# Reordered loads, a second pair of decay buffers and a split last accumulation in a fused state-space scan and feed-forward kernel on one Trainium2 core

## The chip, the cores and the metric

The kernel runs on one core of one Trainium2 chip. The time is device microseconds (us) of one execution; the figure of a kernel is the median of its runs. The engines of the core run side by side, each through its own list of instructions in order: PE (TensorE, matmuls and transposes), DVE (VectorE), ACT (ScalarE), POOL (GpSimd) and SP (SyncE, which here only issues transfers). ACT and POOL issue transfers too, as instructions in their own lists. They wait for each other with semaphores.

## The reference

Two blocks follow each other. The first is a scan with decay (4 batches, 8 heads, 768 positions, 32 values a head, state size 16), the second a feed-forward block with 3072 tokens, width 256 and 2048 hidden values:

```python
for c in range(nc):
    xc, Bc, Cc = (x[:, :, sl], B[:, :, sl], C[:, :, sl])
    la = log_a[:, :, sl]
    cum = np.cumsum(la, axis=-1)
    L = np.exp(cum[:, :, :, None] - cum[:, :, None, :]) * causal
    M = np.einsum('bhin,bhjn->bhij', Cc, Bc) * L
    y_intra = np.einsum('bhij,bhjd->bhid', M, xc)
    y_inter = np.einsum('bhin,bhnd->bhid', Cc, state) * np.exp(cum)[:, :, :, None]
    y[:, :, sl] = y_intra + y_inter
    Bx = np.einsum('bhjn,bhjd->bhjnd', Bc, xc) * decay_from_j[:, :, :, None, None]
    state = decay_full[:, :, None, None] * state + np.sum(Bx, axis=2)
x = y.transpose(0, 2, 1, 3).reshape(B * S, H * D)
h = x @ w_in
out = (h * (1.0 / (1.0 + np.exp(-h)))) @ w_out
```

`w_in` and `w_out` arrive as 64-bit floats.

## The kernel before, in words

**Units and pairs.** The 3072 tokens are cut into 12 units of 256 tokens (three to a batch), and the units into 6 pairs. A unit is first scanned: that gives `XF`, its 256x256 input of the feed-forward block. The first pair (units 0 and 1) then goes through the feed-forward block with plain fp32 matmuls on 256 columns (`f_s1`, line 508, and `f_s2`, line 521). Pairs 1 to 5 go through it with operands split in three (`h`, `l` and `d` parts, matmuls of lines 536, 544, 576, 577 and 590) in 80 steps (`step`), 16 to a pair, while the next pair is scanned in between.

**The steps of a scan.** For unit u: `f_T` or `f_TP` transpose B and C (`f_TP` on PE, into one of two PSUM tiles of the tag `h`); `f_T2` makes `ce` on ACT; `f_P` makes `PFX`, the running product of the decays along a chunk of 64, from the tile `pz` (scan on DVE, line 328); `f_C` makes `CW` = transposed C times `PFX` (line 391), which is the last reader of the PSUM tile of `f_TP`; `f_E1` or `f_Ek` make the decay matrix `E` (line 341) from `ab`; `f_B` makes `BT`; `f_G` and `f_D0` are small matmuls (419, 407); `f_S`, `f_SM` carry the state; `f_M` multiplies `E` by the products; `f_Y` and `f_X` (459, 468, 478) give `XF`.

**The decays.** Units 0 and 1 get `ab` by a matmul (`f_Ab`) and `pz` from `pa01`, a broadcast load clamped by `f_P0`. From unit 2 on both are broadcast loads from two arrays in DRAM, `a_in` and `a_zero`, that the kernel itself writes: `acl` holds all decays, `f_A2` clamps them on DVE (265), copies them with a zero column to `acz` (266, 267) and stores both (268, 269). The first column of `a_in` is stored early (274). `load_pa` (line 105, one transfer) and `load_ab` (line 112, four transfers) read them back. There is one `pz` tile for all units.

**The weights.** 16 tiles of 512 KB (`raw`, line 185; 8 of `w_in`, 8 of `w_out`) go through six buffers, `quad`. Each becomes fp32 in five steps: `w_size` on ACT (191, 194), `w_bits` on DVE (199, 201, 202) and an add on POOL (207), which gives `w32`. Tile n may be loaded once `w_bits(n-6)` has read its buffer.

**The order.** The order in which instructions are written is the order on each engine. It is written out by hand: the calls from line 641 on for units 0 and 1, then the table `steps`, whose rows read (unit, weight tile, what to do after that `f_s1`): `b5` is `w_bits(5)`, `s6` is `w_size(6)`, `r11` loads tile 11, `2:T` is the transposing of unit 2, `2:C12B` its `f_C`, `f_E1` twice and `f_B`, and so on. The hidden values of `f_s1` leave the two PSUM tiles `h` by a Silu on ACT (`gT`, 511). All loads but `bn` of unit 0 are issued by SP, in one list; a tiny transfer `mark` (255) holds tile 5 back until tile 3 has landed.

**The end.** `step(80)` to `step(82)` finish the last pair: `s2` (576, 577) adds to the two accumulators `OA[P][0]` and `OA[P][1]`, `s2_d` (590) to `B2`; `f_sum2` (598, ACT) reads `B2`, `f_end` (622, DVE) joins them, and `store` transposes (633) and stores (635) on SP and ACT.

Of the kernel before, what the change touches and what calls it, by code (L numbers as in the profile page):

```python
# [33 lines left out]
def kernel(  # L34
# [48 lines left out]
    sc.tile([128, 40], FP32, name="pad")  # L83
# [15 lines left out]
    ab, bn, tbc, xt = ({} for _ in range(4))  # L99
# [4 lines left out]
    def load_pa(u, q):  # L104
        q.dma_start(out=pz.rearrange("p c t -> p (c t)"),
                    in_=a_in[:, 4 * u:4 * u + 4].rearrange("h (o c) t -> h o (c t)", o=1).to_broadcast([H, N, 4 * Q + 4]))
# [7 lines left out]
    def load_n(u, i, q):  # L114
        b, t0 = at(u)
        if i == 0:
            t = bn[u] = (block("bn0")[:, 0:256].rearrange("p (k h n) -> p k h n", k=2, h=H) if u < 2 else
                         loads.tile([128, 2, H, N], FP32, name="bn"))
        else:
            t = tbc[u] = block("tbc0")[:, 0:256].rearrange("p (k h n) -> p k h n", k=2, h=H)  # L120
        for k in range(2):
            q.dma_start(out=t[:, k], in_=(B, C)[i][b, :, t0 + 128 * k:t0 + 128 * k + 128].rearrange("h p n -> p h n"))  # L122
# [111 lines left out]
    pa01 = block("pa01")  # L234
    pz = const.tile([128, 4, Q + 1], FP32, name="pz")
    one = const.tile([128, 4, Q + 1], FP32, name="one")
    load_t(0, 1, nc.sync)
    load_n(0, 0, nc.scalar)
    nc.sync.dma_start(out=pa01, in_=bass.AP(tensor=a.tensor, offset=a.offset, ap=[[S, H], [0, N], [1, 2 * UT]]))
    load_x(0, nc.sync)  # L240
    for n in range(3):
        load_w(n, nc.sync)
# [4 lines left out]
    acl, acz = (block(n).rearrange("p (h t) -> p h t", t=Q) for n in ("acl", "acz"))  # L247
# [4 lines left out]
    mark = const.tile([1, RAW - 5], U32, name="mark")  # L252
    for n in range(3, RAW):
        if n > 4:
            nc.sync.dma_start(out=mark[:, n - 5:n - 4], in_=raw[n - 2][0:1, 0, 0, 0:1])
        load_w(n, nc.sync)

# [4 lines left out]
    def f_A2():  # L262

        r = slice(0, NC0 * batch)
        nc.vector.tensor_scalar(out=acl[r], in0=acl[r], scalar1=1.0, scalar2=1e-6, op0=ALU.min, op1=ALU.max)
        nc.vector.tensor_copy(out=acz[r], in_=acl[r])
        nc.vector.memset(acz[r, :, 0:1], 0.0)
        nc.sync.dma_start(out=a_in[:, :, 1:].rearrange("h c t -> c h t"), in_=acl[r])
        nc.sync.dma_start(out=a_zero, in_=acz[r])
# [4 lines left out]
    nc.sync.dma_start(out=a_in[:, :, 0:1].rearrange("h c t -> c h t"),  # L274
                      in_=misc[:NC0 * batch, 0:H].rearrange("p (h t) -> p h t", t=1))
# [17 lines left out]
    nc.vector.memset(pz[:, :, 0:1], 0.0)  # L293
    nc.vector.memset(one, 0.0)
    nc.vector.memset(one[:, :, 0:1], 1.0)
    for c in range(2):
# [5 lines left out]
    ident = const.tile([128, 128], FP32, name="ident")  # L302
    nc.vector.memset(ident, 0.0)
    nc.gpsimd.affine_select(out=ident, in_=ident, pattern=[[-1, 128]], compare_op=ALU.not_equal,
                            fill=1.0, base=0, channel_multiplier=1)

    diag = const.tile([128, H, Q], FP32, name="diag")
    nc.vector.tensor_copy(out=diag, in_=diag1.to_broadcast([128, H, Q]))
# [5 lines left out]
                            fill=0.0, base=N - 1, channel_multiplier=-1)  # L314
    par = const.tile([128, 2], FP32, name="par")
# [6 lines left out]
    def f_P0(u):  # L322
        src = pa01[:, UT * u:UT * u + UT].rearrange("p (c t) -> p c t", t=Q)
        nc.vector.tensor_scalar(out=pz[:, :, 1:], in0=src, scalar1=1.0, scalar2=1e-6, op0=ALU.min, op1=ALU.max)

    def f_P1(u):
        PFX[u] = sc2.tile([128, 4, Q + 1], FP32, name="pfx")
        nc.vector.tensor_tensor_scan(out=PFX[u].rearrange("p c t -> p (c t)"),
                                     data0=pz.rearrange("p c t -> p (c t)"),
                                     data1=one.rearrange("p c t -> p (c t)"), initial=0.0,  # L330
                                     op0=ALU.mult, op1=ALU.add)

    def f_P(u):
        if u < 2:
            f_P0(u)
        f_P1(u)
# [25 lines left out]
    def f_B(u, engine=nc.vector):  # L362
        BT[u] = sc.tile([128, 2, H, N], FP32, name="BT")
        engine.tensor_tensor(out=BT[u], in0=bn[u], in1=E[u][:, :, :, Q - 1:Q].to_broadcast([128, 2, H, N]),
                             op=ALU.mult)
# [23 lines left out]
    def f_C(u):  # L389
        CW[u] = sc.tile([128, UT], FP32, name="cw")  # L390
        nc.vector.tensor_tensor(out=CW[u].rearrange("p (c t) -> p c t", t=Q),  # L391
                             in0=CT.pop(u).rearrange("p (c t) -> p c t", t=Q), in1=PFX[u][:, :, 1:], op=ALU.mult)
# [6 lines left out]
    def f_D0(u):  # L399
        last = u % UPB == UPB - 1  # L400
        bt = BT.pop(u).rearrange("p k h n -> p k (h n)")
        xc = xt[u].rearrange("p k h d -> p k (h d)")
        d = [new_dp(u)[:, c, 256:384].rearrange("p (k x) -> p k x", k=2) for c in range(2)]
        for t in range(3 if last else 4):
            k, c = divmod(t, 2)
            for g in range(4):
                nc.tensor.matmul(out=d[c][32 * g:32 * g + 32, k],  # L407
                                 lhsT=bt[64 * c:64 * c + 64, k, 32 * g:32 * g + 32],
                                 rhs=xc[64 * c:64 * c + 64, k, 64 * g:64 * g + 64], start=True, stop=True,
                                 tile_position=(64 * c, 32 * g), skip_group_check=True)  # L410
        BX[u] = d

# [154 lines left out]
    def s2(s):  # L567
# [5 lines left out]
        gh, gl = GH.pop(s), GL.pop(s)  # L573
        for m in range(2):
# [65 lines left out]

    f_T(0, 1)
    for e in range(2):
        f_T2(0, e)
    f_Ab(0, 0)
# [4 lines left out]
    busy(2, 10)  # L649
    f_Ek(0, 0)  # L650
    f_Ek(0, 1)
    f_B(0)
    f_D0(0)
    f_P(0)
    f_C(0)
# [8 lines left out]
    busy(3, 18)  # L664
# [13 lines left out]
    w_bits(2, 2)  # L678
    f_P(1)
    f_C(1)  # L680
    f_G(1)
# [8 lines left out]
    for n in range(6, 9):  # L690
        load_w(n, nc.sync)
    load_bcx(2)
# [6 lines left out]
    load_pa(2, nc.sync)  # L699
    load_ab(2, nc.sync)  # L700
    load_w(10, nc.sync)
    load_bcx(3, "cx")
    w_size(5)

    def stage(u, what):
        for c in what:
            if c == "L":
                load_unit(u)
            elif c == "A":
                load_pa(u, nc.sync)  # L710
                load_bcx(u, "b")
                load_ab(u, nc.sync)
# [39 lines left out]
    def todo(text):  # L752

        for step in text.split():
            if ":" in step:
# [6 lines left out]
    steps = ((1, 0, ""), (0, 3, "b5 r11 s6"), (1, 1, "b6 s7"), (1, 2, "b7 s8"), (1, 3, "b8"), (0, 4, "2:T"),  # L762
             (1, 4, "2:P"), (0, 5, "2:C12B s9 3:A r12 r13"), (1, 5, "2:D b9 r14 r15 s10"), (0, 6, "2:SsM"), (1, 6, "b10 s11"),
             (0, 7, "2:Y b11 s12 3:T"), (1, 7, "3:PC12B b12 s13 h0 l0"))
# [3 lines left out]
    for text in ("m0 3:D 4:L 3:SsM 2:h h1 l1 2:l 2:d d0 b13 s14", "m1 3:Y 3:h h2 l2 d1 b14 s15", "m2 3:l 3:d d2 b15 h3 l3",  # L768
                 "m3 p0 d3 h4 l4 4:T", "m4 h8 l8 d4 h5 l5 d8", "m5 d5 h9 l9 d9"):
        todo(text)  # L770
# [14 lines left out]
    def step(s):  # L785
# [14 lines left out]
        if s == last + 1:  # L800
            s2(t)
# [3 lines left out]
        if s == last + 2:  # L805
            s2(t)
            f_end(NP - 1)
            return
# [11 lines left out]
        if t >= 0 and not ends:  # L820
            s2(t)
# [58 lines left out]
```

## Time and profile before

| | |
|---|---|
| time, median of 3 runs (lowest, highest) | 338.35 us (338.19, 340.29) |
| the profiled execution: its time | 339.9 us |
| its span | 338.0 us |
| mean granted TensorE clock in it | 0.986 |
| PE busy | 322.8 us (96%) |
| DVE busy | 252.4 us (75%) |
| ACT busy | 218.6 us (65%) |
| POOL busy | 69.1 us (20%) |
| moved by DMA | 30.87 MB, mean 91 GB/s |

The span is the time between the first and the last instruction that the profiler saw; 1.9 us of the profiled execution lie around it. All start times below are counted from the start of the span. A busy PE is not a PE at its peak: at a lower granted clock the same matmuls are busy for longer.

### The profile page before, as it was taken

The numbers are of one execution on the slowest core, as the hardware profiler recorded it, in microseconds if no ns is written. First come the engines' busy times: TensorE is split into PE (matmuls) and PEld (weight loads), VectorE is DVE, ScalarE is ACT, GpSimd is POOL, SyncE is SP. The second block draws the span as 40 slices with busy tenths as digits, with TensorE's granted clock in tenths as the row PEclk, the third lists the DMA queues.
The fourth block names the chain that finished last, engine by engine and source line by source line (L and its number), as shares of the span: only waits on it lengthen the run. The fifth ranks groups of instructions, "written<-read, shape, count | busy, mean of one in ns | idle before, by whom it ended". The sixth has DMA issues, their size and how long they took to land.

```text
span 338.0 us, 7790 instructions
## 1 busy us (share of the span) xinstructions
PE 322.8 (96%) x3145; PEld 256.4 (76%) x3146; DVE 252.4 (75%) x420; ACT 218.6 (65%) x417; POOL 69.1 (20%) x66
## 2 busy tenths in 40 slices
PE   8879599999999999999999999999999999999992
PEld 4558478888878778778788778788778788888881
DVE  7998558997677888996965996865996854674443
ACT  3656535956478898767666666767667756666651
POOL 3226313257001222231202230202240202000000
PEclk9999969999999999999999999999999999999998
DMA  6968878795674584154330154420343000020003
GB/s 127 224 211 211 191 185 206 222 170 108 114 150 67 101 157 89 46 112 75 71 78 0 50 107 85 101 40 0 66 104 52 2 2 0 0 49 17 0 2 62
DMA packets 97290, 30.87 MB, mean 91 GB/s; under 512 B 82230, under 2 KB 88374, under 8 KB 97254
## 3 DMA queue, kind: packets, MB, share of 16 engines
q1 hardware_dynamic: 90758, 25.78, 34.1%
q0 software_dynamic: 2304, 4.20, 7.2%
q10 hardware_dynamic: 4192, 0.39, 0.9%
q8 instruction: 25, 0.41, 0.5%
q14 instruction: 11, 0.09, 0.1%
HBM read 22.82 MB, written 3.34 MB: 77 GB/s over the span
## 4 chain that ended last, share of the span: by engine, by line
PE 85%; SPq 8%; DMA 4%; DVE 1%; issue 1%; ACT 0%; DVEq 0%; ACTq 0%
PE hp L544 23%; PE b L590 11%; PE hp L536 11%; PE oa L576 11%; PE oa L577 11%; PE oa L521 8%; PE hp L508 4%; SPq L122 4%; DMA raw<-in_moe_w_in_dram 3%; PE gy L468 2%; PE gy L419 2%; PE gy L459 2%; DMA pz<-a_in 1%; PE gy L407 1%; SPq L185 1%; SPq L145 1%
## 5 line engine op out<-in xcount | busy, mean ns | idle before, releaser
L538 ACT ACTIVATE hp<-hp 128x512 f32<-128x512 f32 x80 | 46.6, 583 | 72.1 <-PE hp L536 72.0
L558 DVE TENSOR_TENSOR gl<-g,gh 128x512 fp32r<-128x512 f32 x62 | 42.7, 689 | 52.2 <-ACT gh L554 49.1
L544 PE MATMUL hp<-xh,wh 128*128 128x512 f32 x160 | 65.2, 407 | 0.0
L562 DVE SCALAR_TENSOR_TENSOR gd<-gh,g 128x512 fp32r<-128x512 f32 x80 | 59.5, 747 | 5.2 <-ACT gh L554 5.2
L544 PE MATMUL hp<-xl,wl 128*128 128x512 f32 x160 | 62.6, 391 | 0.0
L576 PE MATMUL oa<-gh,wh 128*128 128x512 f32 x160 | 62.5, 391 | 0.0
L577 PE MATMUL oa<-gl,wl 128*128 128x512 f32 x160 | 62.4, 390 | 0.0
L558 POOL TENSOR_TENSOR gl<-g,gh 128x512 fp32r<-128x512 f32 x18 | 29.2, 1623 | 121.9 <-ACT gh L554 121.9
L554 ACT ACTIVATE gh<-g 128x512 fp32r<-128x512 f32 x80 | 50.5, 632 | 2.8
L536 PE MATMUL hp<-xd,wd 128*128 128x512 f32 x160 | 49.5, 391 | 0.0
L552 ACT ACTIVATE g<-hp 128x512 f32<-128x512 f32 x80 | 47.5, 593 | 0.5 <-PE hp L544 0.5
L590 PE MATMUL b<-gd,wd 128*128 128x512 f32 x160 | 44.4, 390 | 0.0
L508 PE MATMUL hp<-xf,w 128*128 128x256 f32 x128 | 32.8, 411 | 5.1 <-DVE cw L391 3.3
L544 PEld LDWEIGHTS hp<-xh,wh 128*128 128x128 f32 x160 | 30.0, 188 | 9.1 <-ACT hp L538 2.5
L536 PEld LDWEIGHTS hp<-xd,wd 128*128 128x128 f32 x160 | 30.0, 188 | 6.7
L576 PEld LDWEIGHTS oa<-gh,wh 128*128 128x128 f32 x160 | 30.0, 188 | 6.4
L590 PEld LDWEIGHTS b<-gd,wd 128*128 128x128 f32 x160 | 30.0, 188 | 6.5 <-DVE o L616 0.3
L577 PEld LDWEIGHTS oa<-gl,wl 128*128 128x128 f32 x160 | 30.0, 188 | 6.3
L508 PEld LDWEIGHTS hp<-xf,w 128*128 128x128 f32 x128 | 25.5, 205 | 11.3 <-issue 3.6
L544 PEld LDWEIGHTS hp<-xl,wl 128*128 128x128 f32 x160 | 30.1, 188 | 5.2
L207 POOL TENSOR_TENSOR w<-wu,wv 128x512 uint32<-128x512 uint32 (+1 forms) x20 | 23.3, 1174 | 45.6 <-DVE wv L202 41.7
L521 PE MATMUL oa<-gT,w 128*128 128x256 f32 x128 | 29.0, 381 | 0.0
(81 smaller groups left out, 375.2 us busy)
## 6 DMA issues: line engine op xcount, KB each, us to landing
ab<-a_zero SPq DMA_DIRECT2D x40, 128.0 KB
raw<-in_moe_w_in_dram SPq DMA_DIRECT2D x8, 512.0 KB
raw<-in_moe_w_out_dram SPq DMA_DIRECT2D x8, 512.0 KB
wl<-w POOLq DMA_DIRECT2D x16, 256.0 KB, 4.2
xt<-in_x_dram SPq DMA_DIRECT2D x24, 128.0 KB
out_dram<-ot SPq DMA_DIRECT2D x44, 64.0 KB
bn<-in_B_dram SPq DMA_DIRECT2D x22, 64.0 KB
tbc<-in_C_dram SPq DMA_DIRECT2D x22, 64.0 KB
```

The costliest lines, as they stand in the source:

```text
L508: nc.tensor.matmul(out=hp[:, i], lhsT=two(w32[j])[:, kc, 128 * i:128 * i + 128], rhs=two(XF[u])[:, kc], start=(kc == 0), stop=(kc == KC - 1))
L521: nc.tensor.matmul(out=OA[0][m][:, UT * u:UT * u + UT], lhsT=two(w32[8 + j])[:, i, 128 * m:128 * m + 128], rhs=two(GT[u, j])[:, i], start= ...
L536: nc.tensor.matmul(out=HP[s], lhsT=two(WD[f // 2])[:, kc, 128 * (f % 2):128 * (f % 2) + 128], rhs=XD[P][:, kc], start=(kc == 0), stop=Fals ...
L538: nc.scalar.activation(HP[s], HP[s], AF.Copy, scale=-HALF / UP)
L544: nc.tensor.matmul(out=HP[s], lhsT=two(w[f // 2])[:, kc, 128 * (f % 2):128 * (f % 2) + 128], rhs=x_[P][:, kc], start=False, stop=(kc == KC ...
L552: nc.scalar.activation(G[s], HP.pop(s), AF.Silu, scale=UP)
L554: nc.scalar.activation(GH[s], G[s], AF.Copy, scale=DOWN)
L558: engine.tensor_tensor(out=GL[s], in0=G[s], in1=GH[s].bitcast(FP32), op=ALU.subtract)
L562: nc.vector.scalar_tensor_tensor(out=GD[s], in0=GH[s].bitcast(FP32), scalar=1.0 + 1.0 / HALF, in1=G.pop(s), op0=ALU.mult, op1=ALU.subtract)
L576: nc.tensor.matmul(out=OA[P][m], lhsT=two(WH[n])[:, r, ms], rhs=gh, start=(f == 0), stop=False)
L577: nc.tensor.matmul(out=OA[P][m], lhsT=two(WL[n])[:, r, ms], rhs=gl, start=False, stop=(f == NF - 1))
L590: nc.tensor.matmul(out=B2[P][:, m], lhsT=two(WD[n])[:, r, 128 * m:128 * m + 128], rhs=gd, start=(fresh and s == tiles[0]), stop=True, skip ...
```

## The change

It has six parts; lines of the new file are a few higher than those of the old one.

1. **Unit 0 and the start.** The load of the decays of units 0 and 1 is split: unit 0's half goes first on ACT's queue, unit 1's half stands after weight tile 0 on SP's. `pz1` is a tile of its own for unit 1. The clamp and scan of unit 0 are done before its C is transposed; unit 0's `f_C` and unit 1's clamp go to POOL, the copy `diag` to ACT, the memset of `ident` to POOL. `f_B` and `f_D0` of unit 0 are done for k = 0 and k = 1 in turn. There are fewer idle matmuls (`busy`).
2. **Decay arrays.** `acz` and its two DVE instructions go: `a_zero` is stored straight from `acl` without its first column. Both stores go to ACT's queue; the first columns of both arrays are stored from POOL.
3. **Loads of unit 2.** C before weight tile 6 on SP, B on ACT's queue after `f_B(1)`, and `pz`, `ab`, x between weight tiles 6, 7 and 8. `mark` goes.
4. **Loads of unit 3.** `pz3` and a `bn` block of its own; both are loaded before `steps`, and `ab` after `f_B(2)`.
5. **`steps`.** Unit 2 is worked on three to four groups earlier, unit 3 two to three; weight steps stand later.
6. **The last pair.** Its last three `s2` do accumulator 0 first, and accumulator 1 of all three afterwards.

```diff
     def load_pa(u, q):
-        q.dma_start(out=pz.rearrange("p c t -> p (c t)"),
+        PZ[u] = pz if u != 3 else block("pz3")[:, 0:4 * Q + 4].rearrange("p (c t) -> p c t", c=4)
+        q.dma_start(out=PZ[u].rearrange("p c t -> p (c t)"),
...
-    nc.sync.dma_start(out=pa01, in_=bass.AP(tensor=a.tensor, offset=a.offset, ap=[[S, H], [0, N], [1, 2 * UT]]))
     load_x(0, nc.sync)
-    for n in range(3):
+    load_w(0, nc.sync)
+    load_a(1, nc.sync)
+    for n in range(1, 3):
         load_w(n, nc.sync)
...
     for n in range(3, RAW):
-        if n > 4:
-            nc.sync.dma_start(out=mark[:, n - 5:n - 4], in_=raw[n - 2][0:1, 0, 0, 0:1])
         load_w(n, nc.sync)
+    load_n(2, 1, nc.sync)
...
-        nc.vector.tensor_copy(out=acz[r], in_=acl[r])
-        nc.vector.memset(acz[r, :, 0:1], 0.0)
-        nc.sync.dma_start(out=a_in[:, :, 1:].rearrange("h c t -> c h t"), in_=acl[r])
-        nc.sync.dma_start(out=a_zero, in_=acz[r])
+        nc.scalar.dma_start(out=a_in[:, :, 1:].rearrange("h c t -> c h t"), in_=acl[r])
+        nc.scalar.dma_start(out=a_zero[:, :, 1:], in_=acl[r, :, 1:])
...
+    def f_A0():
+        for t in (a_in[:, :, 0:1].rearrange("h c t -> c h t"), a_zero[:, :, 0:1]):
+            nc.gpsimd.dma_start(out=t, in_=misc[:NC0 * batch, 0:H].rearrange("p (h t) -> p h t", t=1))
...
+    f_P0(0, nc.vector)
+    f_P(0)
     f_T(0, 1)
     for e in range(2):
         f_T2(0, e)
+    f_C(0, nc.gpsimd)
+    f_P0(1, nc.gpsimd)
+    f_A0()
...
     f_G(0)
-    busy(2, 10)
     f_Ek(0, 0)
+    f_B(0, slice(0, 1))
+    f_D0(0, (0, 1))
+    busy(1, 10)
     f_Ek(0, 1)
-    f_B(0)
-    f_D0(0)
-    f_P(0)
-    f_C(0)
+    f_B(0, slice(1, 2))
+    f_D0(0, (2, 3))
...
     f_B(1)
-    w_bits(2, 2)
+    load_n(2, 0, nc.scalar)
     f_P(1)
     f_C(1)
+    w_bits(2, 2)
...
     f_A2()
-    for n in range(6, 9):
-        load_w(n, nc.sync)
-    load_bcx(2)
+    load_w(6, nc.sync)
+    load_pa(2, nc.sync)
+    load_ab(2, nc.sync)
+    load_w(7, nc.sync)
+    load_x(2, nc.sync)
+    load_w(8, nc.sync)
...
-    load_pa(2, nc.sync)
-    load_ab(2, nc.sync)
     load_w(10, nc.sync)
     load_bcx(3, "cx")
+    load_pa(3, nc.sync)
+    load_bcx(3, "b")
...
-    steps = ((1, 0, ""), (0, 3, "b5 r11 s6"), (1, 1, "b6 s7"), (1, 2, "b7 s8"), (1, 3, "b8"), (0, 4, "2:T"),
-             (1, 4, "2:P"), (0, 5, "2:C12B s9 3:A r12 r13"), (1, 5, "2:D b9 r14 r15 s10"), (0, 6, "2:SsM"), (1, 6, "b10 s11"),
-             (0, 7, "2:Y b11 s12 3:T"), (1, 7, "3:PC12B b12 s13 h0 l0"))
+    steps = ((1, 0, ""), (0, 3, "b5 r11 s6"), (1, 1, "2:PTC1"), (1, 2, "b6 r12 s7 2:2Ba"), (1, 3, "b7 r13 s8"),
+             (0, 4, "2:DSsM"), (1, 4, "b8 r14 s9"), (0, 5, "2:Y b9 r15 s10"), (1, 5, "3:TPC"), (0, 6, "3:12B s11"),
+             (1, 6, "b10 s12 h0 l0"), (0, 7, "3:DSsM 2:h"), (1, 7, "b11 s13"))
...
         if s == last + 1:
-            s2(t)
+            s2(t, (0,))
             s2_d([t, t + 1])
             f_sum2(NP - 1)
             return
         if s == last + 2:
-            s2(t)
+            s2(t, (0,))
+            for i in range(LAG):
+                s2(last - LAG + i, (1,))
             f_end(NP - 1)
```

## The prediction
> **What bounds the kernel now.** I read the page's forty slices first, then the chain of waits, then PE, SP, DVE and ACT in order of time. In the slices, PE is full from the sixth on and its clock falls once:
>
> ```profile
> PE   8879599999999999999999999999999999999992
> PEclk9999969999999999999999999999999999999998
> ```
>
> From 43 us to 331 us the chain is PE alone. Time can be won before 43 us, in the slow clock behind it, and at the end. PE in order of time (start, duration):
>
> ```profile
> 25.43 8.90 PE L508 MATMUL hp<-xf,w 128*128 128x256 f32 x40 [0.47 <-ACT xf L478]
> 35.04 1.97 PE L508 MATMUL hp<-xf,w 128*128 128x256 f32 x8 [0.71 <-ACT gT L511]
> ...
> 42.96 6.44 PE L508 MATMUL hp<-xf,w 128*128 128x256 f32 x16 [3.28 <-DVE cw L391]
> ...
> 50.31 5.45 PE L508 MATMUL hp<-xf,w 128*128 128x256 f32 x24
> ```
>
> PE stands 3.28 us for `cw` of unit 2, because the PSUM tile of the transposed C is free only after it. The next 16 matmuls take 6.44 us, where 24 take 5.38 us in the chain (1.79 per group of 8, so 3.58 for 16): 2.86 us more. The windows of 2 us show why (after the length: busy time of PE, PEld, DVE, ACT, POOL; then the granted clock, DMA share, GB/s):
>
> ```profile
> 40.00:42.00 2.00, 0.00 (x0) 0.00 (x0) 0.44 (x1) 0.32 (x1) 0.00 (x0) 0.93 0.99 260
> 42.00:44.00 2.00, 1.04 (x3) 0.89 (x4) 1.87 (x4) 0.00 (x0) 0.00 (x0) 0.50 0.97 240
> 46.00:48.00 2.00, 2.00 (x6) 1.56 (x5) 0.07 (x1) 1.25 (x3) 0.00 (x0) 0.50 0.76 145
> ```
>
> So this stall costs 3.28 + 2.86 = 6.1 us. DVE and SP show its source:
>
> ```profile
> 41.56 0.70 DVE L328 TENSOR_TENSOR_SCAN pfx<-pz,one 128x260 f32<-128x260 f32 x1 [3.63 <-DMA pz<-a_in]
> ```
> ```profile
> 28.88 6.07 SPq L122 DMA_DIRECT2D bn<-in_B_dram  x2
> 35.05 1.15 SPq L145 DMA_DIRECT2D xt<-in_x_dram  x2
> 36.31 0.88 SPq L185 DMA_DIRECT2D raw<-in_moe_w_out_dram  x1
> 37.23 0.64 SPq L105 DMA_DIRECT2D pz<-a_in  x1
> ```
>
> `a_in` was stored at 23.68, but its reader is issued at 37.23: it stands behind tiles 6 to 9 and the loads of unit 2 in SP's list. The DMA engines are not the limit (share 0.71 to 0.89 between 10 and 60 us, and 24 GB/s in one slice near 33 us).
>
> The end: PE is done at 331.3, and the tail hangs on ACT's sum.
>
> ```profile
> 330.45 1.09 ACT L598 ACTIVATE sum<-b 128x512 f32<-128x512 f32 x2 [3.33 <-PE b L590]
> ```
>
> [...] line 201 takes 0.43 us alone and 1.38 beside POOL's line 207.
>
> **The change part by part.** Times are of the profiled execution (339.9 us, span 338.0), 1.55 above the median of the runs; I subtract the gain from the median.
>
> *Ceiling of the stretch.* From 25.43 to the first line 544 at 82.98 are 57.55 us. PE's work in it: 13 groups x 1.79 = 23.3; `f_s2` 3.45 + 3.65 + 7.10 + 6.91 = 21.1; G and D0 0.98 + 1.01; Y 1.41 + 1.29; one `f_TP` 0.85; line 536 0.46. Sum 50.4, so 7.1 us are lost, 6.1 of them above. None of this work is removed.
>
> *Start (part 1).* DVE loses behind unit 0's second E: clamp 0.28, scan 0.70, `cw` 0.42; the first two reappear in front of E, where DVE waits 0.76 for `hm` and where `hm` now comes before `ident`. `diag` (0.43), `ident` (0.17) and unit 1's clamp (0.29) leave DVE, as do 0.42 + 0.07 in part 2. Half of `f_B` goes before the second E; two small instructions for one, at most +0.1. Sum on DVE about 0.9 earlier at unit 1's M. But XF of unit 1 is made on ACT, behind two new transfer issues there (0.32 each, as SP's rows 268 and 269) and `w_size(4)`: I take 0.3 of 0.9. ACT's `diag` (0.6 as line 511) is hidden beside the wait of 2.02 for `ct`. POOL is idle 8.60 us before 13.15: `f_C`, clamp, and two stores of 4-byte items fit (0.9 to 1.0 per issue as line 220; at POOL's 1.6 against DVE's 0.7 in line 558, `f_C` costs 1.0). If they don't fit, `w32` of tile 0 and with it PE are late: -0.9 to +1.0, taken 0.3 gain. [...] Moving `w_bits(2)` behind P and C of unit 1 (0.7 to 1.13, and 0.42) makes group (0,2) up to 1.3 late, hidden because Y of unit 1 waits for DVE's M then (1.33).
>
> *Loads of unit 2 (parts 2, 3).* On ACT, B's two issues take 1.09 (row ACTq L122), inside ACT's wait of 2.52 before `sm`. ACT issues the `a_in` store at about 23.5. Landing: SP's last output store (issue ended 334.7) had landed by 338.0, so at most 3.3 us: at 26 to 27 SP is let past `pz`. Tiles 3 to 6 and C are ahead in the DMA engines; without `mark` (3.3 us of SP's waiting, 23 GB/s from 21 to 22.5) they go back to back, tile 6 by about 27. So `pz` lands by 27 + 2 to 4.3 (4.3 is its value now, behind a tile) = 29 to 31. DVE reaches its scan behind `w_bits(5)` at about 29, scan and `cw` end 31 to 32.5. PE wants that PSUM tile when group (1,2) is done: 25.1 + 3 x 1.79 + 0.85 + 1.79 = 33.1. **The stall goes**; its cover is about 1 us. The four `ab` (2.41 to issue) land by 32 to 33; E 2 x 1.2, `w_bits(6)` 1.6 to 2.4 between, BT 0.42: 36 to 37, against PE's arrival behind G at 36.7 + 0.6 = 37.3: 0.
>
> *What is late next.* Tile 7 is issued after `ab`, at about 29.5, tile 8 after x at about 31; at 4.3 to 4.5 each (tile 3: 16.91 to 21.24) they land at 34 and 36 to 37. `w_size(7)` and `w_size(8)` stand on ACT in front of the Silu of the group before last, and with two `h` tiles PE waits for that. Silu of (0,4) ends 38.5 to 40 against PE's need at 39.5. I take 0.7 us of new waits, ends 0 and 3. [...]
>
> *Unit 3 and `steps` (parts 4, 5).* `pz3`, two `bn`, four `ab`, x and C have landed by about 45, E of unit 3 runs from about 46. ACT has some 22 us of work in the 27 us of the groups, DVE about 23: cover, but thin. From m0 on, DVE has `w_bits(11..15)` still to do (5 x 1.6 to 2.4), PE 21.1 us of `f_s2`: hidden. Taken 0.3, ends 0 and 2.
>
> Sum: 6.1 + 0.5 (half of the other 1.0) + 0.3 - 0.7 - 0.3 = 5.9 us.
>
> *The end (part 6).* From the last line 544 (325.82) 24 matmuls remain, 0.227 each. `b` needs all its own and what stands before it: 20 now (ends 330.37), 16 after: 0.91 earlier. `gd` of the last tile (328.44) is ready at that place. ACT's sum, DVE's `o` and transpose follow one another; PE still ends at 331.3, before the second `o` wants it (331.5). Gain 0.9.
>
> Total 6.8: span 331.2, profiled execution 333.1, against the median 338.35 - 6.8 = **331.5**.
>
> **The rivals.**
> *A (0.70):* as above, 329.0 (7.1 + 0.9 + 0.9 and a little) to 333.5.
> *B (0.17): half is given back.* ACT's waits for tiles 7 to 10, or DVE beside POOL, open new PE gaps of 3 to 4 us in several pieces. For it: ACT is strictly in order and all weights move later. Against: 20% spare in the stretch. 335, within 334 to 336.
> *C (0.07): slower, SP stuck behind the stores.* If the store of `a_in` lands T later than 27, everything behind `pz` in SP's list is T later. With 0.7 of cover, PE loses T - 0.7[...]. It decides from T = 4.6 (6.8 gone); T = 8 gives 8 - 0.7 + 2.9 - 6.8 = +3.4: 341.8. For it: 4-byte and 252-byte items, a wait never seen here. Against: the output stores landed within 3.3.
> *D (0.06): it doesn't do it.* The stall stays, with another last release (`bn` or `pz` as late): only the end's gain, 337.5.
>
> **How the numbers follow.** 1% is 3.4 us (below 334.97, above 341.73), about what a measurement tells apart. Faster: A and over half of B, 0.81. Same: the rest of B, D and the mild part of C, 0.13. Slower: 0.06. The range 329 to 336 leaves out C, D and some 0.05 of A's and B's edges.
>
> **What would show it.** Right: no wait of line 508 on `cw`, clock 1.00 from 42 to 48 us, `pz` issued near 27, line 544 first near 77, ACT's sum 0.9 us closer behind PE. Wrong: a PE gap at groups (1,4) or (0,5) behind ACT and a weight DMA, SP held past 30 us at `pz`, or a second dip in the clock.

## The result, and the profile after

| | before | after |
|---|---|---|
| median of 20 runs each, side by side | 338.88 us | 341.07 us |
| lowest, highest | 337.17, 343.15 | 339.06, 343.89 |
| span of the profiled execution | 338.0 | 340.4 |
| PE's first split matmul (line 544, after 550) | 82.63 | 85.58 |
| mean granted TensorE clock | 0.986 | 0.988 |

The ratio is 1.0062 (95% interval 1.0037 to 1.0088): a little slower, inside 1%, where 331.5 us was predicted. The row of the first split matmul holds the answer: up to PE's first split matmul (the texts of the experiments call it the first scatter) 2.95 us are lost; from there to the end 0.55 us are won.

The forty slices of the changed kernel, PE and its clock:

```profile
PE   7877994999999999999999999999999999999993
PEclk9997999899999999999999999999999999999999
```

The old dip in slice 6 is gone. In its place there are two: one in slice 4 (25.5 to 34 us) and a hole in PE in slice 7 with a milder dip behind it. PE in order of time names both (start, duration; in brackets the idle time before, and what ended it):

```profile
27.26 7.13 PE L514 MATMUL hp<-xf,w 128*128 128x256 f32 x24 [2.37 <-ACT xf L484]
35.08 5.45 PE L514 MATMUL hp<-xf,w 128*128 128x256 f32 x24 [0.25 <-ACT gT L517]
...
59.24 0.65 PE L411 MATMUL gy<-xt,BT 64*32 64x64 f32 x32 [4.48 <-DVE BT L368]
59.82 3.44 PE L514 MATMUL hp<-xf,w 128*128 128x256 f32 x8
```

The wait of 3.28 us for `cw` is gone, as forecast: the second line waits 0.25 us, for a Silu. **Gap 1** is the first line: PE stands 2.37 us for `XF` of unit 1, where it stood 0.47, and the 24 matmuls behind it take 7.13 us at a granted clock of 0.66 from 28 to 30 us and 0.50 from 30 to 32 us, where 24 take 5.45 at 1.00 (the second line). **Gap 2** is the third: 4.48 us for `BT` of unit 3, then 3.44 us for 8 matmuls at 0.50 from 60 to 62 us (1.99 at 1.00). Behind gap 1 the clock costs 1.7 us, behind gap 2 about 1.5.

ACT ahead of gap 1. `ACTq` is the issue of a transfer in ACT's list:

```profile
23.60 0.50 ACTq L273 DMA_DIRECT2D a_in<-acl  x1
25.55 0.67 ACTq L274 DMA_DIRECT2D a_zero<-acl  x1
26.27 0.66 ACT L192 ACTIVATE wu<-raw 128x512 f32<-128x512 f32 x1 [2.16 <-DMA tbc<-in_C_dram]
26.84 0.65 ACT L484 ACTIVATE xf<-gy 128x256 f32<-128x256 f32 x2
```

Line 192 is the first half of tile 4's size. The bracket puts ACT's 2.16 us down to the load of C, though the instruction reads tile 4; and the issue of the `a_zero` store, ahead of it in the list, began 1.45 us after the other store's had ended. Two suspects then stand ahead of `XF`: the store and tile 4. Before, the same size ran at 24.10 without a wait and `XF` at 25.00.

Gap 2, first in SP's list, then on DVE:

```profile
35.02 4.33 SPq L186 DMA_DIRECT2D raw<-in_moe_w_out_dram  x3
...
42.29 3.35 SPq L146 DMA_DIRECT2D xt<-in_x_dram  x2
45.69 1.57 SPq L106 DMA_DIRECT2D pz<-a_in  x1
...
50.84 2.41 SPq L113 DMA_DIRECT2D ab<-a_zero  x4
```
```profile
51.31 0.42 DVE L395 TENSOR_TENSOR cw<-ct,pfx 128x256 f32<-128x256 f32 x1
56.39 2.34 DVE L344 TENSOR_TENSOR_SCAN E<-ab,diag 128x512 f32<-128x512 f32 x2 [4.65 <-DMA ab<-a_zero]
```

DVE had everything for `E` of unit 3 but `ab`, whose four loads SP issued only from 50.84 on: they stand behind tiles 8 to 10, C, x, `pz` and B of unit 3 and two more tiles. `E` begins 10 us after the forecast 46.

The end went as worked out:

```profile
332.86 1.09 ACT L606 ACTIVATE sum<-b 128x512 f32<-128x512 f32 x2 [2.42 <-PE b L598]
```

ACT waits 2.42 us there instead of 3.33.

### The profile page after: what moved, and what is told of

The parts are those of the page before. It is cut to its first block, busy times and chain, and to the rows that moved or that the text cites. A ratio compares the mean times of both kernels' runs of the same rounds, so it can differ in the third digit from the quotient of the medians.

```text
span 340.4 us, 7774 instructions
## 1 busy us (share of the span) xinstructions
PE 322.7 (95%) x3136; PEld 256.8 (75%) x3136; DVE 251.7 (74%) x416; ACT 219.0 (64%) x418; POOL 71.4 (21%) x71
## 3 DMA queue, kind: packets, MB, share of 16 engines
HBM read 22.82 MB, written 3.34 MB: 77 GB/s over the span
## 4 chain that ended last, share of the span: by engine, by line
PE 83%; DMA 5%; SPq 5%; DVE 3%; ACT 1%; issue 1%; DVEq 0%; ACTq 0%
PE hp L550 23%; PE b L598 11%; PE hp L542 11%; PE oa L584 10%; PE oa L585 10%; PE oa L527 8%; PE hp L514 3%; SPq L123 2%; PE gy L474 2%; PE gy L465 2%; DMA tbc<-in_C_dram 2%; PE gy L425 2%; DMA ab<-a_zero 1%; DMA pz<-a_in 1%; DVE E L344 1%; SPq L186 1%
## 5 line engine op out<-in xcount | busy, mean ns | idle before, releaser
L344 DVE TENSOR_TENSOR_SCAN E<-ab,diag 128x512 f32<-128x512 f32 x24 | 28.4, 1209 | 4.8 <-DMA ab<-a_zero 4.7
```

The lines of the kernel that those rows point to most:

```text
L344: nc.vector.tensor_tensor_scan(out=E[u].rearrange("p k h t -> p (k h t)")[:, Q * g0:Q * (g0 + n)], data0=t.rearrange("p g t -> p (g t)"), ...
```

## The experiments

Each row is a profiled span, the first split matmul in it, and the ratio of the medians to the kernel before (95% interval).

| | built on | span | first split matmul | ratio |
|---|---|---|---|---|
| e1_stores_behind_xf | after | 339.5 | 84.80 | 1.0081 (1.0054 to 1.0109) |
| e2_ab3_on_pool | after | 335.4 | 80.37 | 0.9967 (0.9947 to 0.9987) |
| e4_tail_alone | before | 335.9 | 81.50 | 0.9990 (0.9969 to 1.0012) |
| e5_pz2_ahead | before | 336.3 | 81.01 | 0.9977 (0.9958 to 0.9997) |
| e6_b2_on_sp | e2 | 334.2 | 79.64 | 0.9910 (0.9883 to 0.9938) |
| e7_stores_on_pool | e2 | 333.9 | 78.92 | 0.9944 (0.9924 to 0.9965) |
| e8_clock_kept | e2 | 335.2 | 80.19 | 0.9948 (0.9925 to 0.9971) |
| e9_unit3_first | e7 | 334.6 | 80.14 | 0.9991 (0.9965 to 1.0017) |
| e10_stores_on_pool_alone | after | 341.1 | 86.22 | 1.0044 (1.0025 to 1.0063) |
| e11_x3_last | e7 | 334.7 | 80.19 | 0.9965 (0.9946 to 0.9984) |
| e12_tiles_later | e7 | 336.1 | 81.58 | 0.9970 (0.9952 to 0.9987) |
| e13_b2_sp_and_pool | e7 | 336.5 | 82.11 | 0.9921 (0.9894 to 0.9949) |
| e14_tiles_on_pool | e7 | 335.3 | 80.47 | 0.9961 (0.9927 to 0.9995) |
| e15_tile4_ahead | e7 | 336.2 | 81.29 | 0.9934 (0.9915 to 0.9954) |
| e16_mark_back | e2 | 338.0 | 82.19 | 1.0024 (0.9996 to 1.0051) |

One profiled execution and the median can differ by more than these edits do: e9's profile is the fastest of its 14 executions, those of e10 and e13 are the slowest of theirs. Single waits vary too. e7, e9, e11 and e12 are the same program up to the load of tile 8, yet PE's wait for `XF` of unit 1 reads 0.47, 0.47, 1.20 and 0.47 us, and its wait for the Silu at some 32 us 0.53, 0.67, 0.40 and 1.47. So a wait read from one trace is good to about 1 us. Each verdict below rests on a named wait first, and on the ratio second.

### Gap 2: a place in SP's list

```diff
-                load_ab(u + 1, nc.sync)
+                load_ab(u + 1, nc.gpsimd)
```

> The changed kernel, but the four loads of ab of unit 3 are issued by POOL instead of SP. Theory (place in SP's list): ab of unit 3 lands at 56.3 us because it stands behind x, pz, B and two weight tiles; POOL can issue it at about 41 to 45 us, it lands by 50, PE's gap of 4.48 us before the small matmuls of line 411 goes with the half clock behind it (8 matmuls in 3.44 us instead of 1.8), and the kernel is about 6 us faster than the changed one (near 335 us). Rival (bandwidth): the DMA engines are full there, ab lands no earlier than 54 or the weights land later instead, and less than 2 us are gained.

The issue on POOL, `E` of unit 3 on DVE, and PE behind it:

```profile
41.55 2.12 POOL L113 DMA_DIRECT2D ab<-a_zero  x4
```
```profile
52.47 2.33 DVE L344 TENSOR_TENSOR_SCAN E<-ab,diag 128x512 f32<-128x512 f32 x2
```
```profile
55.32 0.46 PE L411 MATMUL gy<-xt,BT 64*32 64x64 f32 x32 [0.16 <-DVE BT L368]
```

No bracket on `E`: it runs as soon as DVE is there, and 4.48 us of PE's wait have become 0.16. The half clock behind it went too (1.00 from 56 to 64 us). The span fell by 5.0 us and the ratio from 1.0062 to 0.9967, clear of both intervals; the median is 337.13, where 335 was forecast. Gap 2 is the place of `ab` in SP's list; this is shown. Gap 1 stayed (2.25 us, then 7.13 us for 24 matmuls).

Do the two gaps add up? This one mends gap 1 alone: both stores on POOL, tile 4's size behind `XF`, `ab` of unit 3 left on SP.

> The changed kernel, with both stores issued by POOL and the first half of tile 4's size behind XF, and nothing else: the four ab of unit 3 stay in SP's list. It says whether the two gaps add up. Theory (they lie in series, and the second is set by SP's list, whose place in time doesn't move with PE): the gap ahead of unit 1's first group falls from 2.37 to 0.5 and its 24 matmuls from 7.13 to 5.4, so PE is 3.5 us earlier at 34 us; but E of unit 3 still begins when ab lands near 55 to 56, so PE's wait for BT of unit 3 grows from 4.48 to 6.5 to 8 us, and the span stays at 339 to 340.5. Rival (SP's list is let go earlier because the stores land earlier and the tiles come free earlier): ab of unit 3 lands 1.5 to 3 us earlier too, the wait stays at 4 to 5.5, and the span is 337 to 338.5.

```profile
58.84 0.68 PE L411 MATMUL gy<-xt,BT 64*32 64x64 f32 x32 [5.30 <-DVE BT L368]
```

Gap 1 fell to 0.47 us, but PE gave part back to Silus (0.31, 1.05 and 0.62 us), came to the line of gap 2 1.2 us earlier (53.5 instead of 54.8), and waited 5.30 us there instead of 4.48: `E` began at 55.98 (56.39 in the changed kernel), and the span was 341.1. The forecast growth (6.5 to 8) was too large, the reading right: the gaps lie in series. Until the second is mended, mending the first gains nothing that the ratios can tell apart (1.0044 against 1.0062, with overlapping intervals).

### Gap 1: which thing held ACT

The first try left both stores on ACT but put them, and tile 4's size, behind `XF` of unit 1.

> The changed kernel, but ACT makes XF of unit 1 before it issues the stores of a_in and a_zero and before the first half of weight step 4. Theory (ACT's list): PE's gap of 2.37 us in front of the first group of unit 1 and the half clock behind it (24 matmuls in 7.13 us instead of 5.38) come from XF standing behind a store that waits in ACT's list; here the gap is under 0.6 us, the clock stays at 1.00 between 27 and 33 us, and the kernel is about 4 us faster than the changed one (near 337 us), less whatever the stores' later landing (about 2 us) takes back at pz. Rival (DMA): the weights are late because the loads of B of unit 2 share the DMA engines with tiles 3 to 5; then the gap only moves to the next group, which needs tile 3's or 4's w32, and the kernel gains under 1.5 us.

```profile
25.12 1.38 ACTq L276 DMA_DIRECT2D a_in<-acl  x1
26.53 1.48 ACTq L277 DMA_DIRECT2D a_zero<-acl  x1
```
```profile
30.95 1.99 PE L517 MATMUL hp<-xf,w 128*128 128x256 f32 x8 [1.96 <-ACT gT L520]
```

`XF` came in time (0.47 us), but ACT then stood in the two store issues (1.38 and 1.48 us), and PE waited 1.96 us for the Silu behind them and 1.81 for `BT` of unit 2, whose `ab` is read from the later store. The wait had only moved. The next took both things off ACT's list ahead of `XF`, on the base of e2:

```diff
-        nc.scalar.dma_start(out=a_in[:, :, 1:].rearrange("h c t -> c h t"), in_=acl[r])
-        nc.scalar.dma_start(out=a_zero[:, :, 1:], in_=acl[r, :, 1:])
+        nc.gpsimd.dma_start(out=a_in[:, :, 1:].rearrange("h c t -> c h t"), in_=acl[r])
+        nc.gpsimd.dma_start(out=a_zero[:, :, 1:], in_=acl[r, :, 1:])
...
-    w_size(4, "u")
     f_Y(1)
     f_X(1)
-    w_size(4, "v")
+    w_size(4)
```

> The kernel of e2_ab3_on_pool, with both stores (a_in, a_zero) issued by POOL in place of ACT, and the first half of tile 4's size (line 192) behind XF of unit 1. Theory (ACT's list is held between 24.6 and 26.3 us by the issue of the a_zero store, and by tile 4): XF starts right behind Y of unit 1, at about 25.2 in place of 27.2, the gap ahead of the first group of unit 1 is 0.5 us in place of 2.25, the 24 matmuls take 5.4 in place of 7.13, and PE is 3.5 us ahead of e2 at 34 us. If nothing bounds PE next, span 332. Rival (what the gap took is owed to the transfers anyway): PE waits 1.5 to 3 us for cw of unit 2 (its pz landed at 32.7 in e2), for BT of unit 2 or behind tile 7 (landed 40.2 in e2), and span is 334 to 336. In either case XF not being earlier would mean that ACT's list is not what holds it.

```profile
25.48 5.45 PE L514 MATMUL hp<-xf,w 128*128 128x256 f32 x24 [0.47 <-ACT xf L484]
...
54.20 0.46 PE L411 MATMUL gy<-xt,BT 64*32 64x64 f32 x32 [1.75 <-DVE BT L368]
```

Gap 1 and its half clock are gone (granted clock 1.00 from 24 to 48 us): PE ends the 24 matmuls some 3.8 us earlier than in e2. But at 54.2 only 1.1 us of it are left: 1.75 us are lost to `BT` of unit 3, behind a `pz` that now lands too late. The rival said that; more on it below. In time e7 is not clear of e2 (0.9944 and 0.9967, with overlapping intervals). To separate the stores from tile 4, e15 puts `w_size(4, "u")` back ahead of `f_Y(1)` and leaves the stores on POOL:

> The kernel of e7_stores_on_pool, with the first half of tile 4's size (line 192) ahead of XF of unit 1 again, as the changed kernel has it; the stores stay on POOL. It separates the two things that stood ahead of XF on ACT. Theory 1 (the issue of the a_zero store alone held ACT): XF starts by 25.3 and the gap is under 0.7 us. Theory 2 (tile 4 itself is late): line 192 waits for tile 4 until about 25 to 25.6, XF starts at 25.8 to 26.3, the gap is 1.0 to 1.6 us. Half of e2's gap of 2.25 would then be tile 4 and the other half the issue behind it. Span 334 to 335.5 in either case.

ACT, and PE behind it:

```profile
25.89 0.66 ACT L192 ACTIVATE wu<-raw 128x512 f32<-128x512 f32 x1 [1.93 <-DMA raw<-in_moe_w_in_dram]
```
```profile
26.87 7.13 PE L514 MATMUL hp<-xf,w 128*128 128x256 f32 x24 [2.13 <-ACT xf L484]
```

Now the bracket names tile 4. With no store on ACT the gap is 2.13 us (1.0 to 1.6 was forecast), against 2.25 with them, less of a difference than one trace can tell. So **tile 4 is late and its size stands ahead of `XF`**: that is enough to make the gap. The theory that the store's issue alone held ACT fell here. What that issue would do without tile 4 no run shows, since none left it ahead of `XF` with tile 4's size behind. In the changed kernel it ended at 26.22 us, so it could have held `XF` until then; why it began so late no view shows.

In time the gap costs nothing here: e15 has it and its half clock, e7 has not, and their ratios are 0.9934 and 0.9944. That fits a bound further on that both share; see below.

Why is tile 4 late? Two candidates. First, B of unit 2 on ACT's queue, 2048 items of 64 bytes, in flight at the same time. e6 loads it through SP behind C (base e2):

> The kernel of e2_ab3_on_pool, with B of unit 2 loaded through SP's queue behind C of unit 2, and no longer through ACT's. There the gap ahead of the first group of unit 1 is 2.25 us (waiting for XF of unit 1) and its 24 matmuls take 7.13 us. Theory (the 2048 items of 64 bytes of B take the DMA engines from tiles 3 and 4 between 19.7 and 26 us, and tile 4, [...] lands late): tile 4 lands some 1.5 us earlier, ACT issues the a_zero store before 25.0, the gap falls under 1.0 us, the 24 matmuls take about 5.5, and PE reaches the first scatter of output tiles 2.5 to 3.3 us earlier: span about 332.5, ratio to e2 about 0.991. Rival 1 (the engines are full with or without B; only the order of bytes counts): the gap is 2 us or more, as the span (335.4). Rival 2 (the gap moves): gap under 1.0, but PE waits as long further on, for cw or BT of unit 2 or behind tile 7: span 334.5 to 336.

```profile
27.60 7.02 PE L515 MATMUL hp<-xf,w 128*128 128x256 f32 x24 [2.43 <-ACT xf L485]
```

The gap is what it was; B is cleared. The ratio, 0.991, is the lowest of the table nevertheless, with gap 1 in its profile, and clear of e2's; its profile shows PE only 0.7 us earlier than e2's at the first split matmul, 0.4 of it small waits at unit 3 (0.16 and 0.27 in e2); the rest stays open. Second, `mark`: it held tile 5 back until tile 3 had landed. In one stretch of one microsecond the kernel before and e2 compare like this (columns as in the prediction; the last three are clock, DMA share, GB/s):

```profile
20.00:21.00 1.00, 1.00 (x4) 0.61 (x4) 0.87 (x3) 0.00 (x0) 0.96 (x1) 1.00 0.91 352
```
```profile
20.00:21.00 1.00, 0.67 (x56) 0.33 (x38) 0.97 (x3) 0.30 (x1) 0.00 (x0) 1.00 0.92 296
```

Before, the three windows from 18 to 21 us read 303, 367 and 352 GB/s, 1022 KB in all: tiles 3 and 4, of 512 KB each, and nothing behind them, for the next reads 35. In e2 tile 5, C and B are under way as well, and the same three windows read 105, 178 and 296. Part of that is a later start: SP came to the issue of tile 3 at 16.91 us before and at 18.32 in e2. e16 starts as late as e2 (18.63) and brings `mark` back (base e2):

```diff
+        if n > 4:
+            nc.sync.dma_start(out=mark[:, n - 5:n - 4], in_=raw[n - 2][0:1, 0, 0, 0:1])
         load_w(n, nc.sync)
```

> The kernel of e2_ab3_on_pool (stores on ACT, tile 4's size ahead of XF), with the transfer mark back in SP's list: tile 5 is again held until tile 3 has landed, and C of unit 2 behind it. In the kernel before, tile 4's size ran at 24.10 without a wait; in e2 ACT had waited for it and for the store's issue until 26.65. Theory (without mark, tile 5 and C of unit 2 share the transfer engines with tile 4 and make it late): tile 4 lands by 22.5, the a_zero store is issued by 24.8, XF starts by 25.6 and the gap is under 1.0 us, 24 matmuls 5.4 to 5.6. What it costs: tile 5 and C of unit 2 are some 2 to 3 us later, so that pz, ab and BT of unit 2 may be late, a wait of 1 to 3 us at 31 to 42 us. Rival (mark is nothing; B on the other queue or the stores are late by themselves): gap 2 us or more. Span 332.5 to 335.5.

One of the windows, then SP, ACT and PE:

```profile
22.00:23.00 1.00, 0.71 (x3) 0.67 (x4) 0.96 (x3) 0.00 (x0) 0.92 (x2) 1.00 0.98 341
```
```profile
22.98 0.67 SPq L264 DMA_DIRECT2D mark<-raw  x1
```
```profile
26.10 0.66 ACT L192 ACTIVATE wu<-raw 128x512 f32<-128x512 f32 x1 [0.33 <-issue]
```
```profile
27.09 5.45 PE L517 MATMUL hp<-xf,w 128*128 128x256 f32 x24 [1.40 <-ACT xf L487]
```

From 20 to 23 us e16 moved 279, 371 and 341 KB, 991 in all, and 76 in the next microsecond; e2 moved 296, 117 and 243 in the same three. So tiles 3 and 4 again come first and alone, and tile 4's size waits for no transfer any more: `mark` does what the theory says. The forecast of the gap (under 1.0) failed: ACT came to it late, because its issue of B of unit 2 now stood until 23.35 and `sm` behind it waited 2.87 us for a DMA. The full clock held: 5.45 us for the 24 matmuls. And the price came in: Silu waits of 0.43 to 1.69 us, 1.67 us for `BT` of unit 3, span 338.0 and a ratio of 1.0024, worse than e2's 0.9967. Tile 4 in time costs tile 5, C and what follows.

e8 leaves the gap as it is and fills it with eight idle matmuls (`busy(8)` behind `f_Y(1)`):

> The kernel of e2_ab3_on_pool, with eight idle matmuls (128x512, bf16, some 0.22 us each, into a PSUM tile that nobody reads) behind Y of unit 1, in the gap of 2.25 us; nothing else is changed. It leaves the gap and takes only the slow clock behind it. Theory (the clock falls to 0.50 because PE is idle there): the clock stays at 0.98 or more from 28 to 33 us, the 24 matmuls take 5.4 us in place of 7.13, PE is 1.7 us ahead of e2 at 34 us, and, as nothing else was later than PE there by more than 0.4 us, the span is 333.7. Rival 1 (the clock falls for a load or a power cause, whatever PE does in the gap): 7.1 us again, span 335.4. Rival 2 (PE is ahead but waits for BT of unit 2 or for tile 7): 5.4 us, a gap of 1 to 1.7 before 45 us, span 334.5 to 335.4.

```profile
27.40 5.45 PE L514 MATMUL hp<-xf,w 128*128 128x256 f32 x24 [0.98 <-ACT xf L484]
```

Clock 1.00 from 24 to 48 us, 5.45 us instead of 7.13: 1.7 us of gap 1 was the clock's. One trace is weak evidence that the clock falls for idleness, since the same kernel doesn't lose it each time. 1.7 us are 0.005 of the span, and 7 of e2's 22 executions read a mean granted clock of 0.996 or more, which leaves no room for that loss. All executions together say more, though the end of the kernel has a part in the mean too: 0.994 or more in 8 of e2's 22 and in 15 of e8's 20. So the clock is lost less often with the idle matmuls, which speaks against a cause that acts whatever PE does. The gain was spent again at `BT` of unit 3 (1.66 us, 0.16 in e2), so the span is e2's, and the ratio (0.9948) is not clear of e2's.

### Behind the gaps: what bounds up to 56 us

e7 and e8 came to unit 3 ahead of its loads. e9 (base e7) puts `pz` and B of unit 3 ahead of tile 8, C ahead of tile 10, and sizes tile 8 a group later; e11 puts only x behind `pz` and B; e12 `pz`, B and C ahead of tile 10, with tiles 10 and 11 sized later on ACT.

> The kernel of e7_stores_on_pool, with pz and B of unit 3 in SP's list ahead of tile 8 (they stood behind tile 10 and x of unit 3), C of unit 3 ahead of tile 10, and the size of tile 8 on ACT one group later. In e7 PE came to line 411 of unit 3 at 52.4 and waited 1.75 us for BT, whose chain began with pz landing at 50.2. Theory (what is left is again a place in SP's list): DVE's scan of unit 3 no longer waits for pz (2.0 us there) nor the transpose for C (1.55), BT of unit 3 is done by 52, the 1.75 us are gone, first scatter 77 to 77.5 (78.92 there), span 332.2, ratio to before 0.988 to 0.990. Rival (the supply as a whole bounds it): 260 KB ahead of tile 8 cost 0.7 to 1.5 us of waits behind tiles 8 and 9 on ACT, and PE waits for gT, or x of unit 3 lands after 52: span 333.5 to 335.

```profile
49.40 0.68 ACT L192 ACTIVATE wu<-raw 128x512 f32<-128x512 f32 x1 [2.79 <-DMA raw<-in_moe_w_out_dram]
```
```profile
51.16 3.72 PE L514 MATMUL hp<-xf,w 128*128 128x256 f32 x16 [2.99 <-ACT gT L517]
```

The wait for `pz` and that for `BT` went; tile 10 was late instead, and PE lost 2.99 us at a Silu behind it. The rival was right.

> The kernel of e7_stores_on_pool, with x of unit 3 behind pz and B of unit 3 in SP's list instead of ahead of them; all weight tiles keep their places. In e7 the two issues of x took 5.58 us (39.8 to 45.4), so pz was issued only by 47.3 and landed at 50.2. Theory (place in SP's list): pz of unit 3 is issued by 42 to 45 and lands 2 us earlier or more, DVE's scan waits under 0.5 us for it (1.99 in e7), BT of unit 3 is done by 52.2, PE's wait of 1.75 us there falls under 0.6, first scatter at 77.3 to 77.9 (78.92 in e7), span 332.5 to 333, ratio to before 0.988 to 0.992. Rival (SP is held at that place by a transfer, whatever stands there): pz is held until 45 to 47 as x was, and x lands after 52, so PE waits 1.5 to 2.5 us for x or BT: span 333.5 to 335.

PE's wait for `BT` went, and 1.66 us for a Silu behind tile 11 came, with 1.20 us left of gap 1: span 334.7, the rival's.

> The kernel of e7_stores_on_pool, with pz, B and C of unit 3 ahead of tile 10 (x behind it), and the sizes of tiles 10 and 11 one to two groups later on ACT, so that no Silu stands behind a tile that has not landed. In e9, where 260 KB were put further ahead and ACT's order was kept, PE waited 2.99 us for a Silu behind tile 10. Theory (both of those waits are places in in-order lists): no wait of PE over 0.7 us between 26 and 60 us, first scatter at 77 to 77.7, span 332 to 333, ratio to before 0.986 to 0.991. Rival (the transfers as a whole are behind): tile 11 or 12 is late for ACT between 52 and 56, or DVE is late with the tiles of w_out, and PE waits 1.5 to 3 us at a Silu or at line 527 for w: span 333.5 to 335.5.

```profile
52.98 3.34 PE L514 MATMUL hp<-xf,w 128*128 128x256 f32 x8 [2.88 <-ACT gT L517]
```

A Silu again, 2.88 us and a half clock behind. In each of e7, e11 and e12 SP then stood for 4.5 to 5.6 us near 40 to 47 us in one pair of issues, whichever stood there: x in e7, B of unit 3 in e11 and e12. e14 asks whether that list or the transfers are full: tiles 9 and 10 are issued by POOL, the bytes unchanged.

> The kernel of e7_stores_on_pool, with weight tiles 9 and 10 issued by POOL in place of SP; the bytes are the same. Between 34 and 47 us SP's list stands in transfer issues (3.5, 1.4, 5.6 us). Theory (SP's list is held; the transfer engines have room): pz of unit 3 is issued 2 us earlier or more, PE's wait of 1.75 us for BT of unit 3 falls under 0.6, span 332 to 333. Rival (the transfer engines are full from 32 to 44 us, whoever issues): SP's issues end earlier but pz of unit 3 lands at 49 or later again, or tile 7 or 8 later, and PE waits 1.5 us or more for BT or a Silu: span 333.5 to 335.

```profile
34.47 1.78 PE L514 MATMUL hp<-xf,w 128*128 128x256 f32 x7 [2.30 <-ACT gT L517]
```

The wait for `BT` of unit 3 went, but POOL's tile 9 (issued at 26.4) went ahead of tile 6, and PE lost 2.30 us to a Silu behind tile 6. `pz` of unit 3 was issued by 45.60 us (47.35 in e7), and yet the first split matmul was 1.5 us later than in e7. Last, e13 joins e6 and e7:

> Three edits on the changed kernel together: ab of unit 3 and both stores issued by POOL (as e7_stores_on_pool), and B of unit 2 in SP's list behind C of unit 2 (as e6_b2_on_sp). e6 and e7 had ratios to before of 0.991 and 0.994. If the supply of unit 3's loads and the tiles up to 50 us bounds (what e9, e11 and e12 point to), the gap ahead of unit 1's first group is 0.5 us, PE waits again 1 to 2 us at line 411 of unit 3 or at a Silu, first scatter 78.5 to 79.5, span 333.5 to 334.5, ratio 0.990 to 0.994, no better than the better of the two. If the two gains add up: no wait over 0.7 us between 26 and 60, first scatter under 77.8, span under 333, ratio 0.986 to 0.989.

2.31 us at a Silu behind tile 6 and 1.82 at `BT` of unit 3, in the slowest of its 11 executions. The ratio, 0.9921 (0.9894 to 0.9949), is not clear of e6's nor of e7's and misses the 0.986 to 0.989 of a sum: the gains do not add up.

Over all seven orders from e7 on with `ab` on POOL (e7, e9, e11 to e15) PE's first split matmul lies between 78.9 and 82.1 us in the profiled executions; none reached the 77 of the prediction. In e9, e11, e12 and e14 the wait that was mended came back at another load. In time e6, e7, e13 and e15 lie together (0.991 to 0.994), though the profiles of e6 and e15 have gap 1 and those of e7 and e13 have not. This fits a supply of tiles and unit loads that is as late as PE up to 56 us (the DMA share, over 4 us at a time, reads 0.89 to 1.00 between 32 and 44 us in e7). That it is the engines' bandwidth, and not the way items queue in them, no run shows: none took bytes away, and in e7 the share falls to 0.54 from 44 to 48 us while SP stands. Another issuer for tiles 9 and 10 (e14) changed which load was late (tile 6, 2.30 us) and won nothing: its ratio is 0.9961, e7's 0.9944, with overlapping intervals. In e2 another issuer saved 5.0 us of span, because the `ab` loads, issued at 41.55 us instead of 50.84, no longer stood behind others in SP's list.

### Before's own stall, and the end

e5 changes the kernel before: `pz` and `ab` of unit 2 directly behind tile 8, ahead of C, B and x.

> The kernel before, with nothing but the loads of pz and ab of unit 2 moved in SP's list ahead of C, B and x of unit 2 (behind tile 8). Theory (place in SP's list makes the stall of the kernel before): pz lands at 34 to 36 us instead of 41.5, PE's wait for cw falls from 3.28 us to under 2, the clock no longer falls to 0.50 behind it, and 3 to 5 us are gained (334 to 336). Rival (the wait only changes its name): C and B of unit 2 are now as late as pz was, PE waits as long at the transposes, and the time stays within 1 us.

DVE and PE:

```profile
38.41 0.68 DVE L328 TENSOR_TENSOR_SCAN pfx<-pz,one 128x260 f32<-128x260 f32 x1
```
```profile
39.64 0.30 PE L377 MATMUL tp<-ident,bn 128*128 128x128 f32 x1 [2.76 <-DMA bn<-in_B_dram]
```

The scan waits for nothing, and PE waits 2.76 and 0.45 us for B instead of 3.28 for `cw`; the half clock follows (0.50 from 42 to 44 us, 24 matmuls 6.88 us). So the place of `pz` was the last release of that stall, not all of its source: with `pz` and `ab` ahead, B behind them is as late. The time stayed within 1 us, as the rival said. e4 puts only part 6 into the kernel before:

> The kernel before with part 6 alone, the last three output steps with accumulator 0 first. Theory (the sum on ACT is what the end hangs on): 0.9 us faster (338.0 against 338.9), ACT's sum starts about 0.9 us nearer to PE's last hidden-layer matmul. Rival (the end is set by the last matmul of accumulator 1 and the stores): 0 to 0.3 us.

ACT waits 2.4 us for its sum instead of 3.3, 0.9 nearer, and the same in the changed kernel. In time it is 0.4 us at the median, which the interval doesn't separate from nothing.

## Why the prediction was wrong, step by step

- **The stall and its clock, -6.1: happened.** No wait for `cw`, clock 1.00 from 42 to 48 us. The `a_in` store was later than forecast: SP was let past `pz` at 30.0, not at 26 to 27, and `cw` ended at 36.5, not 32.5. It cost nothing, since PE was late itself; in e7, where PE was on time, it waited 0.53 us there, for a Silu. The clock's part (2.86) is that of one execution: in e4's profile the same stall, 3.54 us long, cost 1.8 (16 matmuls in 5.38 us).
- **"XF of unit 1 is made on ACT, behind two new transfer issues there (0.32 each) and `w_size(4)`: I take 0.3 of 0.9": failed**, the first of two. `w_size(4)` was counted as an instruction, not as a wait for tile 4. Taking `mark` away was counted as transfer time won ("they go back to back"); what it protected, tile 4's landing ahead of `XF`, was not asked for. It measured 1.9 us of gap and 1.7 us of half clock in the profile, in place of a gain; in time e7 and e15, without it and with it, don't differ.
- **"Unit 3 and steps: `pz3`, two `bn`, four `ab`, x and C have landed by about 45 ... Taken 0.3, ends 0 and 2": failed**, the second and larger. The sum counted the work of DVE and ACT between 46 and 56 us, but did not walk SP's list up to `ab`: it was issued from 50.84 to 53.25. It measured 4.48 us and about 1.5 us of clock; e2 removed both by another issuer.
- **"The DMA engines are not the limit": this premise of both is not borne out.** It was read off means over 10 us, while the prediction's own windows show a share of 0.99 and 0.97 from 40 to 44 us. The nearly idle stretch that it names (31 and 11 GB/s from 33 to 35 us) is a time in which SP stood in the issue of B of unit 2 (until 34.95), so it doesn't show that loads could have come sooner. e5, e9, e11, e12 and e14 each mended one wait, and it came back at another load. Whether the engines or the lists are full stays open.
- **No clock lost behind waits shorter than before's 3.28 us: failed.** The sum counts none there; that was the author's estimate. Behind 2.37 us of idle PE, with 1.33 us idle some 4 us earlier, the granted clock was 0.50 from 30 to 32 us, and behind other waits below 3.28 us it fell as well (last section).
- **Start, -0.3: did not come.** `Y` of unit 0 is at 12.20 instead of 11.82, 0.4 later. No run took the start apart.
- **New waits of tiles 7 and 8, +0.7: did not come.** ACT did wait for both tiles (0.77 and 1.18 us in the changed kernel, 1.60 and 0.99 in e7), but PE waited for no Silu behind them. The Silu waits of that time (0.25 us, 0.53 in e7, 0.67 in e9) stand behind tile 6.
- **The end, -0.9: right** for ACT's wait; from the first split matmul to the end of the span 0.55 us are won.

No rival named the two gaps. B had the kind (ACT's waits for tiles), with the wrong tiles and less than half the size. C had SP held at `pz` until 30, inside its mild part; that its 341.8 is close to the measured 341.07 is chance. The sum fails by what was added, not by what was removed: -6.1 for the stall with its clock and -0.55 at the end, against +3.6 for gap 1, +6.0 for gap 2 and +0.4 at the start make +3.3 in the two profiles, where the spans differ by 2.4; of the rest 0.5 is the Silu wait of before (0.71, now 0.25). Mending what was added doesn't bring the forecast back: the best ratio of all orders, 0.991 (e6), is a median of 335.94, some 4 us above it. What PE waits for then, in the traces, is loads that are late up to 56 us.

## What to carry to other kernels

When loads are moved ahead, walk the issuing engine's whole list in order of time up to the last load that the next stage needs, and ask for each tile whose load is moved or let go earlier what now lands later. An instruction that is the first reader of a load is a wait in its engine's list, whatever its own duration (tile 4's size, 0.66 us long, waited 1.93 us in e15); put it behind the instruction that another engine is waiting for. A transfer that only holds others back may be what keeps an urgent one in time (with `mark` back, tile 4's size waited for no transfer in e16).

## What the runs showed of the hardware that was not expected

- **Half clock, not by the length of one wait alone.** Behind 2.13 us (e15) and 2.37 us (after) of idle PE, each with 1.33 us idle shortly before, 24 matmuls took 7.13 us, where they took 5.45 at a granted clock of 1.00; behind 1.81 us in e1, 16 took 5.41 us (clock 0.50 from 44 to 46 us), and behind 2.88 us in e12, 8 took 3.34 (0.59 and 0.56 in the windows from 52 to 56 us). Behind 2.99 us in e9, 16 took 3.72 us (1.00 from 50 to 56 us), and behind 2.31 us in e13, 24 took 5.45. Executions of one kernel differ as well: e2's mean granted clock lies between 0.986 and 0.999. What decides it no run shows; in these traces a wait was not safe for being shorter than the 3.28 us of before's stall.
- **A transfer's issue can hold its engine.** ACT's issue of the `a_zero` store took 0.67 us but began 1.45 us after the end of the one ahead of it, and two such issues took 1.38 and 1.48 us in e1. On POOL the same two took 0.73 and 0.64 us without a wait between them (e7). What holds an issue no view shows.
- **A store that another load reads back** let SP pass 4.8 to 6.4 us after its issue (23.6 to 30.0 in the changed kernel, 23.7 to 28.5 in e7); in the changed kernel 3.1 us of that are SP's wait for the store at `pz`.
